# Retention attention and two expert layers on one core: attention's chunk loads held behind the first, decode steps spread later, blend operands in other slots

## The chip, the core and the metric

The kernel runs on one NeuronCore of one Trainium2 chip. The core has a matrix engine (TensorE, "PE" in the profile, with its weight loads as "PEld"), VectorE ("DVE"), ScalarE ("ACT"), GpSimd ("POOL") and SyncE ("SP", which here only issues DMAs). Sixteen DMA engines carry the transfers that the queues of SP, ACT and POOL ask for. Each engine runs its own instruction stream in order; semaphores order the engines among each other. The metric is the device time of one execution in microseconds (us). Three executions of the kernel before took 986.65, 987.84 and 989.09 us.

## The reference, cut to what matters

```python
# attention: 4 batches, 8 heads, 768 tokens, head size 64
for t in range(S):
    state = gamma * state + einsum('bhd,bhe->bhde', k[:, :, t], v[:, :, t])
    y[:, :, t] = scale * einsum('bhd,bhde->bhe', q[:, :, t], state)
x = y.transpose(0, 2, 1, 3).reshape(B * S, H * D)      # 3072 x 512
# first expert layer: w1, w2 are 512 x 1024, w3 1024 x 1024, w_out 1024 x 512
h = (x @ w1) * (x @ w2) @ w3
x = (h @ w_out).astype(float32)
# second: w_in 512 x 2048, w_out 2048 x 512
h = x @ w_in
out = (h * sigmoid(1.702 * h)) @ w_out
```

The weights come as 64-bit floating point numbers.

## The kernel before, in words

**Arithmetic.** Every large product is made of three matmuls in the fast 32-bit format (`mm3`, L245 to L248). Each operand is held as a high part and a low part, the remainder: high x high, high x low, low x high. So each operand needs a cast to its high part on ACT (line L261) and a subtraction for its low part on DVE (L162). The larger products are done in seven block products instead of eight, with sums and differences of blocks as operands.

**Stages, in the order of time.**
- *Attention*: 24 chunks of 128 tokens (four batches of six). A chunk's input is a tile `qkv` with q and k (`qk`) and k and v (`kv`). `scores` makes s (L354), `masked` makes pt on DVE (L366), `updates` and `next_state` hold the running state (the copy on ACT is L392), `outputs` makes y (L404), which DVE turns into xb (L426) and which is split into xh and xl. `load(c)` asks for a chunk: chunk 0's and 1's qk go out on SP's queue (L333), their kv and all later chunks on POOL's (L334, L336). In the preamble the loads of chunks 0 to 5 are asked for one after the other.
- *Gates*: six blocks of 512 tokens (n = 0 to 5), each with eight gates (t = 0 to 7). A gate multiplies a block of x with one tile of w1 and w2 (24 matmuls), and ACT and DVE multiply both results (L284, L285) to a tile of h, which goes to DRAM (`hd`); in n = 3 to 5 with its sums and differences b and g (L1009 to L1015). n = 0 runs among attention's chunks. The x of the next block is reloaded (`reload`) and split in four pieces d = 0 to 3 (`split_x`) during the present one. Among the gates of n = 1 and 2 lie eight "mixes", in which w3 and w_out are multiplied with each other.
- *Blend*: 21 turns, three token blocks times seven products, each 24 matmuls, with h as the operand and the mixed weight; a turn's operand is one megabyte from `hd`, loaded by `load_h` (L790) into a tile l0 to l3, then cast to `h` (ACT) and reduced to its low part (DVE).
- *Expand*: four token blocks by eight tiles of w_in, with the gelu; the left operands (`op`) come from DRAM (`sp`), two tiles each (high and low), in the places that `SLOT` gives them.
- *Contract*: 21 turns that end in the stores to `out`.

**Weights.** A weight tile comes from DRAM as two raw tiles of 64-bit numbers (`fetch`, L118, five buffers). ACT takes its magnitude (L128), DVE rebuilds the 32-bit number in steps (L183 to L205), ACT and DVE split it, or POOL makes sums of it (`seven`, L159). `weight_steps` is a generator with ten such steps a tile; `work(n)` runs the next n. It is called with a number after every gate, every mix and in the first turns of blend, so that the decoding lies between the other instructions of DVE and ACT. An earlier fetch is held by a small memset on DVE (L117) into the raw tile, which the DMA must wait for.

**What sets the order.** Everything is issued in the order of the program text, per engine. Tiles come from pools; a tile that takes another's place waits until that one's last reader is through. The blend's four tiles l0 to l3 lie where the gate stage's last tiles lay: the first on the staging tiles `st`, the second on both `b12`, the third and fourth on the two tiles `g`. The last gates of n = 5 ("opening", L665 on) also load and split what blend's turns 0 and 1 start with.

Of the kernel before, what the change touches and what calls it, by code (L numbers as in the profile page):

```python
# [43 lines left out]
def tile_kernel(  # L44
# [225 lines left out]
    def split_x(key, d):  # L270
        hi, lo = (t[:, d] for t in xhl[key])
        split(hi, lo, lo.bitcast(F32))
# [29 lines left out]
    class Attention:  # L302
# [18 lines left out]
                    t, dyt[0], self.step[:, c].to_broadcast([P, KD, P]), ALU.mult  # L321
                )

        def load(self, c):
            if c in (4, 5):
                qk, kv = (
                    homes["wg"].tile([P, 1024], F32, tag="wg", bufs=16, name=f"c{x}") for x in "qk"
                )
            else:
                t = self.tile("qkv", 2048, 4)  # L330
                qk, kv = t[:, :1024], t[:, 1024:]
            if c in (0, 1, 4, 5):
                (nc.sync if c < 2 else nc.gpsimd).dma_start(qk, qkv[c][:, :1024])  # L333
                nc.gpsimd.dma_start(kv, qkv[c][:, 1024:])  # L334
            else:
                nc.gpsimd.dma_start(t, qkv[c])  # L336
            qkt[c] = qk.rearrange("p (a n t) -> p a n t", a=2, n=NP)
            kvt[c] = kv.rearrange("p (a h d) -> p a h d", a=2, h=H)
# [172 lines left out]
    left = {}  # L511
    PART = dict(P1=0, P2=1, P4=2, P5=3, P6=4, P7=5, P3=6)

    SLOT = "e", 0, 1, 4, 2, 3, 5, 6
    pools = {True: spare}

    def slot(n, shape):
# [207 lines left out]
    def contract(p, ps):  # L725
        def add(out, x, y):
            nc.vector.tensor_tensor(out, x, y, ALU.add)

        def store(x, h, i, q, value):
            t = p.tile([P, TB], F32, tag="o", bufs=4, name="c")  # L730
            add(t, *value)
            at = 0
            while at < TB:
                s, t0 = divmod(i * TB + at, TS)
                m = min(TB - at, TS - t0)
                to = s * 2 * TS + h * TS + t0
                rows = slice((2 * x + q) * P, (2 * x + q + 1) * P)
                nc.sync.dma_start(out[rows, to : to + m], t[:, at : at + m])
                at += m

        u = [p.tile([P, 3, 2, TB], F32, name="ua")]
        for n, (name, i) in enumerate(turns):
            r = n // 3
            load_turn(n + 2, p)
            if i == 0 and r + 1 < 7:
                load_w(turns[n + 3][0], (6, 4)[r % 2], nc.gpsimd if r else nc.sync)
            if name == "P5" and i == 0:
                u += [slot(x, [P, 3, 2, TB]).bitcast(F32) for x in (2, 3)]
            pq = [ps.tile([P, TB], F32, tag="m", bufs=6, name="m") for _ in range(2)]
            for q in range(2):  # L750
                for k in range(NQ):
                    mm3(
                        pq[q],
                        *(t[:, k, q * P : (q + 1) * P] for t in ws[name]),
                        high[n][k // KH][:, k % KH],
                        low_of(n, k),
                        k == 0,
                        k == NQ - 1,
                    )
            split_turn(n + 1, p)  # L760
            if i == 1 and r + 1 < 7:
                split_w(turns[n + 2][0], (7, 5)[r % 2])
            for q, m in enumerate(pq):
                ua, p5, u4 = (t[:, i, q] for t in (u * 3)[:3])
                if name == "P1":
                    nc.scalar.copy(ua, m)
                if name == "P2":
                    store(0, 0, i, q, (m, ua))
                if name == "P6":
                    add(ua, m, ua)  # L770
                if name == "P5":
                    nc.scalar.copy(p5, m)
                    add(u4, ua, p5)
                if name == "P3":
                    store(0, 1, i, q, (m, u4))
                if name == "P7":
                    add(ua, m, ua)
                    store(1, 1, i, q, (ua, p5))
                if name == "P4":
                    store(1, 0, i, q, (m, ua))  # L780
# [6 lines left out]
    def load_h(n, a, b, t):  # L787
        i, name = blends[n]
        lo2.setdefault(n, []).append((a, b, t))
        nc.sync.dma_start(t.bitcast(F32), hd[i][:, a:b, RIGHT[name]])  # L790
# [17 lines left out]
    def opening(t):  # L808
        if t:
            name = blends[t - 1][1]  # L810
            wm[name] = wtile("wg")
            nc.sync.dma_start(
                wm[name][1].bitcast(F32), sm[PART[name]].rearrange("p k c -> p (k c)")
            )
        if t == 1:
            x = spare.tile([P, 7, TB], F32R, tag="ope", name="h0")
            hi2[0] = x[:, NM:]
            load_h(0, 0, NM, x[:, :NM])
        if t == KF - 2:
            for k in (0, 2):  # L820
                load_h(1, k, k + 2, prep.tile([P, 2, TB], F32R, tag="r", bufs=R_BUFS, name="h1"))
        if t in (3, 4, 5):
            split_h(0, t - 3, t - 2, hi2[0][:, t - 3 : t - 2])
        if t == 6:
            hi2["k3"] = prep.tile([P, TB], F32R, tag="x", bufs=6, name="h3")
            split_h(0, 3, 4, hi2["k3"].rearrange("p (a t) -> p a t", a=1))
        if t in (4, 6):
            split_wm(t // 2 - 2)

    def blend(p, ps, todo):  # L830
# [4 lines left out]
        def tile(kind, bufs):  # L835
            return p.tile([P, NM, TB], F32R, tag=kind, bufs=bufs, name=kind)
# [13 lines left out]
        def store(i, e, t):  # L850
            nc.gpsimd.dma_start(yd[i][:, e], t)

        ls = {n: tile(f"l{n % 4}", 1) for n in range(2, 6)}
        for n in (2, 3):
            load_turn(n)
        held = [p.tile([P, TB], F32, tag="o", bufs=2, name="c")]
        hi2[1] = tile("h", 2)
# [48 lines left out]
    with tc.manual_schedule():  # L906
# [4 lines left out]
        with (  # L911
# [8 lines left out]
            nc.sync.dma_start(attention.step[:, :NCK], cstep)  # L920
            attention.factors(0)
            for c in range(2, 6):
                attention.load(c)
            attention.factors(1)
            gates = 0
            late = []
# [7 lines left out]
                gates += 1  # L934

            def fill(c, at):
                for _ in range({(0, 0): 2, (3, 0): 2, (4, 0): 1}.get((c, at), 0)):
                    fetch(held=True)
                if c > 1:
                    work(PACE.get(c, (1, 1, 2, 1))[at])  # L940
                if (c, at) == (CPB + 1, 2):
                    magnitude(1)
                while late:
                    gate_first(*late.pop())
                if c in range(13, 17) and at == 1:
                    reload(ORDER[1], c - 13)
                if c in range(17, 21) and at == 3:
                    split_x(ORDER[1], c - 17)
                if at == 3 and c > CPB + 1 and gates < min(complete, KF):
                    first_gate()  # L950
# [7 lines left out]
        with (  # L958
# [63 lines left out]
            for n, i in list(enumerate(ORDER))[1:]:  # L1022
                nxt = ORDER[n + 1] if n + 1 < NB else None
                for t in range(KF):
# [7 lines left out]
                    if n >= 2 and nxt is not None and t == KF - 2:  # L1032
                        load_b(nxt, 0)
                    ab = gate_mm(t, i, gate_tile)
                    if nxt is not None and t >= KD:
                        split_x(nxt, t - KD)
                    work(((8, 6, 3, 3)[n - 1] + (n < 4) * (t % 2)) if n < 5 else (t < 4) + (t < 5))
                    (gate_second if n > 2 else gate_first)(t, i, ab)
                    while rows < KF and (complete > W3 + rows or (n, t) == (2, KF - 1)):
                        ps = mix_mm(rows)  # L1040
# [149 lines left out]
```

## Time and profile before

| | us |
|---|---|
| three runs, median | 987.84 |
| the profiled execution | 987.63 |
| its span (first to last instruction) | 985.8 |
| PE busy | 965.2 (98%) |
| DVE busy | 716.9 (73%) |
| ACT busy | 444.4 (45%) |
| POOL busy | 200.6 (20%) |

The stages begin at: attention 0, gates of n = 1 138, n = 2 226, n = 3 271, n = 4 316, n = 5 362, blend 405, Expand 521, contract 750. A row of the timeline gives start and duration, the engine, the line, the operation, output <- input, and in brackets how long the engine was idle before, and on whom it waited. PEclk is the TensorE clock granted, as a share of 2.4 GHz; 0.50 is the lower level of 1.2 GHz. The three runs spread over 2.4 us.

### The profile page before, as it was taken

The numbers are of one execution on the slowest core, as the hardware profiler recorded it, in microseconds if no ns is written. First come the engines' busy times: TensorE is split into PE (matmuls) and PEld (weight loads), VectorE is DVE, ScalarE is ACT, GpSimd is POOL, SyncE is SP. The second block draws the span as 40 slices with busy tenths as digits, with TensorE's granted clock in tenths as the row PEclk, the third lists the DMA queues.
The fourth block names the chain that finished last, engine by engine and source line by source line (L and its number), as shares of the span: only waits on it lengthen the run. The fifth ranks groups of instructions, "written<-read, shape, count | busy, mean of one in ns | idle before, by whom it ended". The sixth has DMA issues, their size and how long they took to land.

```text
span 985.8 us, 14859 instructions
## 1 busy us (share of the span) xinstructions
PE 965.2 (98%) x5608; PEld 836.6 (85%) x5608; DVE 716.9 (73%) x966; ACT 444.4 (45%) x786; POOL 200.6 (20%) x243
## 2 busy tenths in 40 slices
PE   5999999999999999999999999999999999999998
PEld 5788878888877888888889999999999888888886
DVE  3878878888898986774886895867777475567662
ACT  4666644442322213445445744545445544354430
POOL 4000000259685875340110000000000000000000
PEclk9999999999999999999999999999999999999999
DMA  8989956669988989998877647455596968767971
GB/s 333 354 321 348 360 195 221 200 218 326 339 302 322 358 311 371 378 315 286 278 238 278 261 168 270 187 223 233 194 358 254 331 230 284 244 197 245 288 232 54
DMA packets 115464, 268.73 MB, mean 273 GB/s; under 512 B 8000, under 2 KB 69568, under 8 KB 106304
## 3 DMA queue, kind: packets, MB, share of 16 engines
q1 hardware_dynamic: 101552, 196.08, 57.7%
q0 software_dynamic: 13840, 71.70, 18.8%
q8 instruction: 44, 0.72, 0.3%
q14 instruction: 28, 0.23, 0.1%
HBM read 165.52 MB, written 102.24 MB: 272 GB/s over the span
## 4 chain that ended last, share of the span: by engine, by line
PE 64%; DVE 2%; issue 0%; ACT 0%; DVEq 0%
PE m L248 12%; PE m L247 12%; PE m L246 12%; PE a L247 4%; PE a L248 4%; PE a L246 4%; PE psm L247 3%; PE psm L248 3%; PE psm L246 3%; PE e L248 2%; PE e L247 2%; PE e L246 2%; PE c L248 1%; PE c L247 1%; PE c L246 1%; DVE g L583 1%
## 5 line engine op out<-in xcount | busy, mean ns | idle before, releaser
L247 PE MATMUL psm<-xl,wh 128*128 128x512 f32 x320 | 125.3, 392 | 2.3 <-DVE xl L162 2.3
L246 PE MATMUL psm<-xh,wh 128*128 128x512 f32 x320 | 125.4, 392 | 0.8 <-ACT xh L261 0.8
L248 PE MATMUL psm<-xh,wl 128*128 128x512 f32 x320 | 125.2, 391 | 0.0
L248 PE MATMUL m<-h,op 128*128 128x512 f32 x320 | 124.5, 389 | 0.0
L246 PE MATMUL m<-h,op 128*128 128x512 f32 x320 | 124.5, 389 | 0.0
L247 PE MATMUL m<-l,op 128*128 128x512 f32 x304 | 118.3, 389 | 0.0
L685 ACT CAST h<-l 128x2048 fp32r<-128x2048 f32 x38 | 72.3, 1915 | 83.3 <-PE m L248 51.3
L686 DVE TENSOR_TENSOR l<-l,h 128x2048 fp32r<-128x2048 f32 x38 | 85.6, 2287 | 21.2 <-ACT h L685 21.2
L247 PE MATMUL a<-yl,op 128*128 128x384 f32 x256 | 85.7, 335 | 0.1
L246 PE MATMUL a<-yh,op 128*128 128x384 f32 x256 | 85.7, 335 | 0.0
L248 PE MATMUL a<-yh,op 128*128 128x384 f32 x256 | 85.6, 334 | 0.0
L691 POOL DMA_DIRECT2D op<-sw x6 | 3.2, 531 | 393.3 <-PE a L248 212.9
L128 ACT ACTIVATE x<-raw 128x512 f32<-128x512 f32 x72 | 46.3, 673 | 74.4 <-DMA raw<-in_wo_dram 40.5
L247 PEld LDWEIGHTS psm<-xl,wh 128*128 128x128 f32 x320 | 60.5, 189 | 15.7 <-DVE xl L162 3.0
L246 PEld LDWEIGHTS psm<-xh,wh 128*128 128x128 f32 x320 | 60.5, 189 | 13.9 <-ACT xh L261 1.2
L248 PEld LDWEIGHTS psm<-xh,wl 128*128 128x128 f32 x320 | 60.4, 189 | 12.5
L246 PEld LDWEIGHTS m<-h,op 128*128 128x128 f32 x320 | 60.1, 188 | 12.4
L248 PEld LDWEIGHTS m<-h,op 128*128 128x128 f32 x320 | 60.1, 188 | 12.4
L247 PEld LDWEIGHTS m<-l,op 128*128 128x128 f32 x304 | 57.1, 188 | 11.9
L246 PE MATMUL m<-h,wh 128*128 128x512 f32 x168 | 65.4, 389 | 0.0
L248 PE MATMUL m<-h,wl 128*128 128x512 f32 x168 | 65.4, 389 | 0.0
L162 DVE TENSOR_TENSOR l<-l,h 128x2048 fp32r<-128x2048 f32 x19 | 43.6, 2293 | 26.2 <-ACT h L261 24.7
(160 smaller groups left out, 2205.2 us busy)
## 6 DMA issues: line engine op xcount, KB each, us to landing
gd<-g SPq DMA_DIRECT2D x32, 1344.0 KB, 4.8
qkv<-in_qkv_dram POOLq DMA_DIRECT2D x20, 1024.0 KB, 8.3
l<-gd SPq DMA_DIRECT2D x26, 768.0 KB, 6.9
l<-hd SPq DMA_DIRECT2D x19, 1024.0 KB, 6.9
raw<-in_w_dram SPq DMA_DIRECT2D x32, 512.0 KB, 5.1
hd<-g POOLq DMA_DIRECT2D x12, 1280.0 KB, 8.8
raw<-in_wo_dram SPq DMA_DIRECT2D x24, 512.0 KB, 6.9
l<-gd SPq DMA_DIRECT2D x24, 512.0 KB, 5.4
```

What stands on the lines that cost most here:

```text
L128: nc.scalar.activation(x, high, AF.Abs, scale=2.0**16)
L162: nc.vector.tensor_tensor(lo, x, hi.bitcast(F32), ALU.subtract)
L246: nc.tensor.matmul(ps, wh, xh, start=start, stop=False, skip_group_check=True)
L247: nc.tensor.matmul(ps, wh, xl, start=False, stop=False, skip_group_check=True)
L248: nc.tensor.matmul(ps, wl, xh, start=False, stop=stop, skip_group_check=True)
L583: nc.vector.tensor_tensor(g[:, x], y, z, ALU.subtract)
L685: nc.scalar.copy(hi, x.bitcast(F32))
L686: nc.vector.tensor_tensor(x, x.bitcast(F32), hi.bitcast(F32), ALU.subtract)
L691: queue.dma_start(t.bitcast(F32), sw[PART[name]])
```

## The change

Seven edits:
1. `load` takes a second argument. For chunk 2 POOL first copies one column of chunk 0's qk into the new tile, so the DMA behind it is asked for when chunk 0's qk has landed.
2. The first two held raw fetches move from the step behind chunk 0's scores to that behind chunk 1's (`fill`).
3. `work` after each gate: in n = 1 to 4 8, 6, 3, 3 steps, without one more at every second gate of n = 1 to 3; in n = 5 3, 3, 3, 2, 2, 0, 0, 0 in place of 2, 2, 2, 2, 1, 0, 0, 0.
4. `split_x` of the next block at t = 3 to 6 in place of 4 to 7.
5. The operand of blend's turn 1 (h1) is no longer loaded into two raw buffers in the opening. The four tiles l are given to turns 1 to 4 in place of 2 to 5, and three turns are loaded at blend's start in place of two.
6. `SLOT`, the places of the left operands in Expand: operand 4 goes to place 5, 5 to 2, 6 to 3.
7. The very last store: the add is made in two parts (128 and 384 columns), each before its DMA, and the second DMA is issued by ACT.

```diff
-        def load(self, c):
+        def load(self, c, behind=None):
...
+                if behind is not None:
+                    nc.gpsimd.tensor_copy(qk[:, :1], behind)
...
-    SLOT = "e", 0, 1, 4, 2, 3, 5, 6
+    SLOT = "e", 0, 1, 4, 5, 2, 3, 6
...
-            add(t, *value)
+            last = (x, h, i, q) == (1, 0, 2, 1)
+            if not last:
+                add(t, *value)
...
-                nc.sync.dma_start(out[rows, to : to + m], t[:, at : at + m])
+                part = slice(at, at + m)
+                if last:
+                    add(t[:, part], *(v[:, part] for v in value))
+                queue = nc.scalar if last and at else nc.sync
+                queue.dma_start(out[rows, to : to + m], t[:, part])
...
-        if t == KF - 2:
-            for k in (0, 2):
-                load_h(1, k, k + 2, prep.tile([P, 2, TB], F32R, tag="r", bufs=R_BUFS, name="h1"))
...
-        ls = {n: tile(f"l{n % 4}", 1) for n in range(2, 6)}
-        for n in (2, 3):
+        ls = {n: tile(f"l{n % 4}", 1) for n in range(1, 5)}
+        for n in (1, 2, 3):
             load_turn(n)
...
-                attention.load(c)
+                attention.load(c, qkt[0][:, 0, 0, :1] if c == 2 else None)
...
-                for _ in range({(0, 0): 2, (3, 0): 2, (4, 0): 1}.get((c, at), 0)):
+                for _ in range({(1, 0): 2, (3, 0): 2, (4, 0): 1}.get((c, at), 0)):
...
-                    if nxt is not None and t >= KD:
-                        split_x(nxt, t - KD)
-                    work(((8, 6, 3, 3)[n - 1] + (n < 4) * (t % 2)) if n < 5 else (t < 4) + (t < 5))
+                    if nxt is not None and t in range(KD - 1, KF - 1):
+                        split_x(nxt, t - KD + 1)
+                    work((8, 6, 3, 3)[n - 1] if n < 5 else (3, 3, 3, 2, 2, 0, 0, 0)[t])
```

The change moves instructions at three places. The first is DVE's queue at the program's start; the memsets on `raw` release the first two fetches of weights. Before:

```order
L366 TENSOR_TENSOR pt<-s,mask 128x512 x2
L117 MEMSET raw 128x2 x2
L366 TENSOR_TENSOR pt<-s,mask 128x512 x2
L426 TENSOR_TENSOR xb<-y,dy 128x512
L162 TENSOR_TENSOR xl<-xb,xh 128x4x128
```

DVE's queue at the same place now:

```order
L368 TENSOR_TENSOR pt<-s,mask 128x512 x4
L428 TENSOR_TENSOR xb<-y,dy 128x512
L162 TENSOR_TENSOR xl<-xb,xh 128x4x128
L117 MEMSET raw 128x2 x2
L368 TENSOR_TENSOR pt<-s,mask 128x512 x2
```

The memsets have moved behind both chunks' masks and the xb and xl of chunk 0.

The second place is DVE's queue in the last two gates of n = 3, where the products that end in L1012 and L1009 belong to gates 5 and 6, and the rows of L162 on xl are the split pieces of the next block. Before:

```order
L1012 TENSOR_TENSOR g<-g,b_3202 128x512
L162 TENSOR_TENSOR xl<-xl,xh 128x512
L191 TENSOR_SCALAR x<-x 128x512
L195 SCALAR_TENSOR_TENSOR x<-raw,x 128x512 x2
L285 TENSOR_TENSOR b_3288<-b_3288,psm 128x512
L1009 TENSOR_TENSOR g<-b_3288,h 128x512
L162 TENSOR_TENSOR xl<-xl,xh 128x512
L205 SCALAR_TENSOR_TENSOR x<-raw,x 128x512 x2
```

DVE's queue now, from gate 4 to the same product of gate 6 (lines are five higher from L1004 on):

```order
L1014 TENSOR_TENSOR g<-b_3173,h 128x512
L162 TENSOR_TENSOR xl<-xl,xh 128x512
L195 SCALAR_TENSOR_TENSOR x<-raw,x 128x512
L205 SCALAR_TENSOR_TENSOR x<-raw,x 128x512 x2
L285 TENSOR_TENSOR g<-g,psm 128x512
L1017 TENSOR_TENSOR g<-g,b_3173 128x512
L162 TENSOR_TENSOR xl<-xl,xh 128x512
L183 TENSOR_SCALAR x<-x 128x512 x2
L191 TENSOR_SCALAR x<-x 128x512
L285 TENSOR_TENSOR b_3264<-b_3264,psm 128x512
L1014 TENSOR_TENSOR g<-b_3264,h 128x512
```

The last xl piece stands behind gate 5's products and no longer behind gate 6's.

The third place is SP's queue at the end of the gates and the start of blend, where the numbers tell apart what has the same name (l1 to l3 are the tiles of blend's operands, wl those of its weights). Before:

```order
L812 DMA wl_3933<-sm0_99 128x1024
L790 DMA h1_3935<-hd0_77 128x2x512
L790 DMA h1_3937<-hd0_77 128x2x512
L812 DMA wl_3976<-sm0_99 128x1024
L790 DMA l2_4022<-hd0_77 128x4x512
L790 DMA l3_4023<-hd0_77 128x4x512
L790 DMA l0_4024<-hd0_77 128x4x512
L790 DMA l1_4025<-hd0_77 128x4x512
L790 DMA l2_4151<-hd0_77 128x4x512
```

SP's queue there now (L798 is the line that was L790, L820 that which was L812):

```order
L820 DMA wl_3914<-sm0_99 128x1024
L820 DMA wl_3953<-sm0_99 128x1024
L798 DMA l1_3999<-hd0_77 128x4x512
L798 DMA l2_4000<-hd0_77 128x4x512
L798 DMA l3_4001<-hd0_77 128x4x512
L798 DMA l0_4002<-hd0_77 128x4x512
L798 DMA l1_4088<-hd0_77 128x4x512
L798 DMA l2_4133<-hd0_77 128x4x512
```

The two halves of h1 are gone, and the four tiles now begin with turn 1's operand.

## Rows read from the trace of the kernel before

**Rows 1.** Windows: length, busy time of each engine, PEclk, DMA share, GB/s

```profile
40.62:981.53 940.91, 936.60 (x5194) 812.54 (x5192) 693.77 (x924) 420.95 (x709) 187.75 (x220) 1.00 0.76 270
318.25:322.00 3.75, 3.75 (x10) 2.93 (x11) 3.71 (x6) 1.16 (x2) 2.46 (x4) 0.54 1.02 425
426.70:443.00 16.30, 16.30 (x73) 13.50 (x72) 12.66 (x11) 7.29 (x5) 7.41 (x11) 1.00 0.95 322
```

**Rows 2.** Waits of PE over the whole span: us in total, times, longest

```profile
PE s L354 <- DMA qkv<-in_qkv_dram: 10.3, 2, 6.0
PE psm L247 <- DVE xl L162: 2.3, 2, 2.0
...
PE psm L246 <- ACT xh L261: 0.8, 1, 0.8
```

**Rows 3.** Timelines of PE, POOL, DVE and ACT, first 25 us

```profile
12.37 2.08 PE L354 MATMUL s<-qkv 64*128 64x128 f32 x16 [6.03 <-DMA qkv<-in_qkv_dram]
...
2.47 1.05 POOL L336 DMA_DIRECT2D qkv<-in_qkv_dram  x2
...
18.63 1.11 DVE L162 TENSOR_TENSOR xl<-xb,xh 128x512 fp32r<-128x512 f32 x1 [0.69 <-ACT xh L261]
...
24.15 1.23 ACT L128 ACTIVATE x<-raw 128x512 f32<-128x512 f32 x2
```

**Rows 4.** DMA from 0 to 7.8: a queue's packets, MB; an issue's landing

```profile
q0 software_dynamic: 267, 1.02, 40.6%
...
ck<-in_qkv_dram POOLq DMA_DIRECT2D x2, 512.0 KB, 17.5
```

**Rows 5.** DMA issues of the page: KB each, us to landing

```profile
raw<-in_w_dram SPq DMA_DIRECT2D x32, 512.0 KB, 5.1
```

**Rows 6.** DMA issues from 27 to 29

```profile
raw<-in_w_dram SPq DMA_DIRECT2D x2, 512.0 KB, 8.9
```

**Rows 7.** Timeline around 318, end of n = 3

```profile
317.48 0.68 DVE L162 TENSOR_TENSOR xl<-xl,xh 128x512 fp32r<-128x512 f32 x1
...
318.22 0.57 PE L247 MATMUL psm<-xl,wh 128*128 128x512 f32 x1 [1.98 <-DVE xl L162]
```

**Rows 8.** Waits of SP's queue, 404 to 423

```profile
SPq L790 <- DVE g L1012: 13.9, 1, 13.9
SPq L790 <- DMA hd<-g: 11.5, 2, 11.2
```

**Rows 9.** Timelines of SP, ACT and DVE, end of the gates and blend

```profile
391.91 0.53 SPq L790 DMA_DIRECT2D l<-hd  x1
...
406.45 1.49 SPq L790 DMA_DIRECT2D l<-hd  x2
...
415.82 0.59 ACT L847 COPY s<-m 128x512 f32<-128x512 f32 x1 [1.56 <-PE m L248]
416.31 1.92 ACT L261 CAST h<-l 128x2048 fp32r<-128x2048 f32 x1
...
418.25 2.29 DVE L162 TENSOR_TENSOR l<-l,h 128x2048 fp32r<-128x2048 f32 x1 [0.75 <-ACT h L261]
...
419.23 0.52 SPq L790 DMA_DIRECT2D l<-hd  x1
...
421.26 0.59 ACT L847 COPY s<-m 128x512 f32<-128x512 f32 x1 [1.62 <-PE m L248]
```

**Rows 10.** DMA issues of 391.5 to 392.5, 404 to 407, 407 to 410, 419 to 419.5

```profile
l<-hd SPq DMA_DIRECT2D x1, 1024.0 KB, 16.0
...
l<-hd SPq DMA_DIRECT2D x1, 1024.0 KB, 6.7
...
l<-hd SPq DMA_DIRECT2D x1, 1024.0 KB, 13.4
...
l<-hd SPq DMA_DIRECT2D x1, 1024.0 KB, 5.5
```

**Rows 11.** Timeline of SP's queue, the end

```profile
982.29 0.81 SPq L738 DMA_DIRECT2D out_dram<-c  x2
```

## Prediction of the time after the change

> **What bounds the kernel now.** I read the page's engine table first, then the waits of PE, the windows, and the timelines around each wait. PE is the engine at its limit. From its first gate at 40.62 us to its last matmul it is busy for 936.60 of 940.91 us [rows 1]. So nothing that makes another engine faster shortens the run, unless PE waits for that engine now, or will. The table of PE's waits [rows 2] says where that can be: 10.3 us for two landings of attention input (4.3 before the first chunk, 6.0 before the second), and 0.8 + 2.3 us in the gates for the two halves of x, xh and xl. A further loss is no wait: behind the longest of these, PE ran at a mean granted clock of 0.54 for 3.75 us [rows 1], which is mostly the lower level of 1.2 GHz, and cost about 3.75 x 0.46 = 1.7 us.
>
> So there are at most some 4.8 us to gain in the gates and the start's landings beside that. Against them stands every place where PE doesn't wait now and the change takes its lead away. The sum goes against the profiled execution, 987.63 us (span 985.8 and 1.8 around it); the median of the runs shown, 987.84, is 0.2 above it.
>
> **x split a gate sooner, with fewer decode steps: -4.8.** The last xl piece of block n = 4 is made by DVE at 317.48, behind two gate products and their decode steps, and PE's first matmul with it starts at 318.22 after 1.98 idle [rows 7]. The change moves that instruction one gate ahead; a gate is 24 matmuls, about 5.4 us (as long as a blend turn, below), more than the 1.98 it was late. It issues no more than before, and the piece that it reads was reloaded two gates or more earlier. The same holds at the start of n = 3, where PE waited 0.77 for xh and 0.31 for xl (0.8 in the table, and 2.3 less 1.98) [rows 2]. The eight decode steps or so that leave the earlier blocks make room on DVE besides. The waits are 3.1, and the slow clock behind the long one is 1.7: 4.8. What is late next at those places is nothing that I find; the next block's edge has no wait today.
>
> Here a rule weighs on the 1.7. The row shows the clock at 0.54 just behind a wait of 1.98, and that is all that this one execution can say. The Trainium skill ("TensorE: Matmul & The Clock Gate", Part 1: The HAM clock gate) holds that the gate watches activity on a free-running beat, so that the same kernel is caught or spared by chance from run to run. By that rule the 1.7 would be missing in some executions of before, and this part would be worth 3.1 there, the whole sum 989.7; I keep the row's value, as the execution that I sum against paid it.
>
> **The first operands of the blend: +4.4.** Before, blend's turn 1 read its operand from two raw buffers loaded during the gates, and the four slots in the new pool served turns 2 to 5. Now those slots serve turns 1 to 4, in the same places, so each operand from turn 2 on gets the slot that the next turn's had. SP's queue shows when these places come free [rows 8, 9]: the first at 391.91; the second and third at 406.45, after SP had stood 13.9 us for the gate stage's last DVE product; the fourth at 419.23, after 11.2 us for the store of g. They landed 16.0, 6.7, 13.4 and 5.5 us later [rows 10]: at 407.9, 413.2, about 420.9 (issued at 407.5) and 424.7.
>
> From landing to use come ACT's cast, 1.92, and DVE's remainder, 2.29 [rows 9]. Turns follow each other at 415.82 and 421.26, 5.44 apart [rows 9].
> - Turn 1: its load no longer has the megabyte of h1 ahead of it, so it lands between 398.6 (7 us, as the faster loads took) and 407.9, DVE can start at 406.4, and it is ready by 408.7 to 412.1, for a turn that begins at 415.82 - 5.44 = 410.4. Cost 0 to 1.7; I take 0, because ahead of it is less than before.
> - Turn 2: lands 413.2, high part 415.1, low part 417.4. Its second matmul needs the low part at 416.0. Wait 1.4.
> - Turn 3: lands 420.9, high 422.8, low 425.1. After turn 2's delay its second matmul would stand at 422.9. Wait 2.2.
> - Turn 4: lands 424.7, low part at 429.0, while it starts at 426.7 + 3.6 = 430.3. No wait.
>
> That is 3.6. The clock may fall behind one of these waits, as it did behind the 1.98, for 1.7 or not at all; I take half, 0.8. Both ends: 0, if the slots come free or the loads land sooner in the new pool; 5.3 with the fall, and with turn 1's 1.7, 7.0. Two more decode steps now lie in each of turns 4 to 7, on tiles as large as an xl piece (0.68 [rows 7]), where DVE is busy for 12.66 of the 16.30 us from 426.7 on [rows 1]; three turns' worth is 4.2 against 3.6 idle. So DVE falls behind there by 0.6 or a little more for a while, but in each turn it makes the next operand ahead of its steps, some 3 us before it is due. No cost.
>
> **The raw fetches at the start: +1.1.** Before, DVE asks for the first two raw weight tiles behind the first masked scores, at 10.1. Now the request stands behind the xl of chunk 0, which ends at 18.63 + 1.11 = 19.7 [rows 3], so the second leaves at about 20.2. ACT reads them in two instructions from 24.15, the second from 24.75, and behind these in its queue stands the copy of the state, for which PE waits. Raw tiles land in 5.1 us in the middle [rows 5], in 8.9 at a crowded place [rows 6], so the second is there at 25.3 to 29.1 and ACT stands 0.5 to 4.3. By then POOL's queue is short: the last half chunk, issued by 5.6, took 17.5 [rows 4] and is in by 23. So I go by the lower row and take 1.1. Less than 0.5 would need a start with nothing else under way.
>
> **Third and later chunks behind the first: 0.** POOL now copies a column of chunk 0 first, so chunk 2's request leaves when that has landed, at about 4.3 (10.3 less 6.0 [rows 2]), and not at 2.47 [rows 3]. But up to 7.8 us POOL's queue had moved 1.02 MB [rows 4], less than the two half-megabytes (1.05 MB) of chunks 0 and 1 that stand before chunk 2 in it. Chunk 2 wasn't under way yet, so it took nothing from chunk 1's landing at 12.37 [rows 3]. Behind the waiting copy stand the later chunk loads alone; the last of them is in by 23 either way, as the queue stays full. Ends: 0.5 lost, if the queue runs dry for a moment, 3.5 gained, if it is really the mere presence of those requests that slows chunk 1.
>
> **The tail: -0.3.** The last add is cut into a quarter and the rest, and the second store goes out on ACT's queue; before, both stores were issued by SP in 0.81 behind the whole add [rows 11]. The second issue, 0.4, now stands beside the first, while a further DVE instruction adds a little. Ends 0 and -0.5. **The other slots** of the left operands cost nothing: the first of them is fetched ahead of Expand and used behind its first products, well after the last blend turn has freed the place.
>
> Sum: 987.63 - 4.8 + 4.4 + 1.1 + 0 - 0.3 = 988.0.
>
> **Rivals.**
> A. The blend isn't late. If the order in which the pools hand out the places lets turns 2 and 3 load 2 us or more sooner, no term of blend is left: 988.0 - 4.4 = 983.6. For it: SP's 13.9 us wait is for a product that moves with the decode load. Against: that product is the last of its stage in either order.
> B. The start gains. Chunk 1 lands up to 3.5 sooner: 984.5. For it: 6.0 us is PE's largest wait, and 1.02 MB by 7.8 is close to the 1.05. The Trainium skill ("DMA: Bandwidth & Descriptors", Queues, rings and completion order) has each DMA engine take packets from its queues in turn, and a queue's in order. By that rule chunk 2 competes only once chunk 1's other half is through, and holding its request back 2 us can't matter while that half is under way: it speaks for 0.
> C. Slower: the raw fetches land late. ACT stands 4.3 at its second raw tile instead of 1.1, the state's copy and PE with it, and the clock falls for 1.7 more: 988.0 + 3.2 + 1.7 = 992.9. It decides from landings over 6 us. For it: that stretch moves chunk inputs at a full share of the engines. Against: the row in the middle.
> D. The split sooner doesn't take the wait away, as ACT's casts are themselves held by raw tiles that come late: 4.8 isn't gained, 992.8.
>
> **How the numbers follow.** Forecast 0.42, A 0.21, B 0.12, C 0.16, D 0.09. What can be told from no change here is about 0.3%, 3 us: 984.9 to 990.8 is the same. The forecast's own range, with blend from 3.6 to 5.3, turn 1 and the tail, is 985 to 991. A is faster nearly whole, B in two thirds, the forecast in a tenth: 0.33. C and D are slower nearly whole, with a tenth of the forecast: 0.27. The same is 0.40. The range goes from 982, past A, to 993, the worse of C and D.
>
> **What would show it.** Right: PE has no wait for xl or xh near 271 and 318 and no half clock there; two waits of 1 to 2.5 us in the blend at its second and third turns, for DVE's l; ACT stands about 1 us at its second raw tile near 25; PE restarts near 12.4 with chunk 1. Wrong: PE restarting before 11.5 (B); blend turns 5.44 apart throughout (A); a PE wait of over 2 us between 25 and 30 (C); psm waits for xl above 0.5 (D).

## The result: 10 us slower, and the profile after

The changed kernel takes 997.45 us in the median of four runs (996.78 to 1000.18), against 987.25 for four of the kernel before (985.85 to 989.09): a ratio of 1.0107, with a 95% interval of 1.0081 to 1.0134. The forecast was 988.0 and its range ended at 993.

The profiled execution took 996.78. From the page of the changed kernel, its span and the row of the engines:

```profile
span 995.0 us, 14853 instructions
...
PE 965.4 (97%) x5608; PEld 835.3 (84%) x5608; DVE 715.6 (72%) x966; ACT 443.9 (45%) x785; POOL 196.9 (20%) x244
```

PE is busy as long as before (965.2) in a span that is 9.2 longer. The waits of PE (us in total, times, longest) say where it stands, and answer to [rows 2]:

```profile
PE s L356 <- DMA qkv<-in_qkv_dram: 8.8, 2, 4.4
PE m L246 <- ACT h L261: 4.5, 1, 4.5
PE y L406 <- DVE xb L428: 3.6, 4, 1.4
PE m L246 <- DVE g L285: 3.1, 1, 3.1
PE m L247 <- DVE l L162: 2.1, 3, 1.5
PE u L382 <- ACT state L394: 1.7, 2, 1.5
```

The rows for xl and xh on psm, the gates' products, are gone, and there are three rows on `m`, the products of blend. Chunk 1's input now costs 4.4 and not 6.0. A table by stages shows it more sharply; its times are those of PE's first matmul of a gate, of blend and of Expand in the timeline, and the span:

| us | to the first gate | gates up to blend | blend | Expand to the end |
|---|---|---|---|---|
| before | 40.6 | 364.1 | 114.2 | 466.8 |
| changed | 41.0 | 358.6 | 128.9 | 466.5 |

Blend without any wait is 21 turns of 5.44, 114.2: before, it had none. So the gates gained 5.5, and blend lost 14.6. The windows of the changed kernel (length, PE busy, then the other engines, PEclk, DMA share, GB/s) show the gain at n = 3 and 4 and the loss at blend's first turns; compare [rows 1]:

```profile
300.00:325.00 25.00, 25.00 (x112) 20.71 (x111) 20.91 (x25) 4.62 (x9) 19.04 (x21) 1.00 0.89 291
402.50:405.60 3.10, 0.00 (x0) 0.00 (x0) 1.29 (x2) 0.59 (x1) 0.00 (x0) 1.00 1.04 436
405.60:410.30 4.70, 4.58 (x12) 3.13 (x12) 0.69 (x1) 0.00 (x0) 3.62 (x3) 0.64 1.00 400
410.30:414.70 4.40, 0.00 (x0) 0.00 (x0) 0.00 (x0) 1.90 (x2) 0.54 (x1) 0.87 1.07 417
414.70:418.00 3.30, 1.72 (x3) 1.11 (x4) 3.27 (x2) 1.92 (x4) 0.00 (x0) 0.50 1.01 420
```

PE stands in the middle of turn 0 and ahead of turn 1, and works at about the lower clock behind both, while the DMA engines are full. Its matmuls' starts give the parts: 3.3 in turn 0 (402.3 to 405.6), 1.7 of slow clock, 4.7 ahead of turn 1 (410.0 to 414.75), 2.1 for its low part, 1.7 of slow clock, 0.9 in two later waits: 14.4 of the 14.6.

The chain that leads there runs over all engines. From the timelines of the changed kernel, 360 to 418 (start, duration, engine, line, output <- input, in brackets the idle time before and its releaser):

```profile
362.53 0.87 SPq L798 DMA_DIRECT2D h<-hd  x1
...
381.93 0.62 ACT L261 CAST h<-h 128x512 fp32r<-128x512 f32 x1 [11.44 <-DMA h<-hd]
...
382.58 0.69 DVE L162 TENSOR_TENSOR h<-h 128x512 fp32r<-128x512 f32 x1 [8.42 <-ACT h L261]
383.19 0.68 DVE L205 SCALAR_TENSOR_TENSOR x<-raw,x 128x512 int32<-128x512 int32 x1
...
383.96 0.85 POOL L159 TENSOR_TENSOR st<-x 128x256 f32<-128x256 f32 x1 [11.59 <-DVE x L205]
...
391.05 1.37 POOL L1018 TENSOR_TENSOR g<-g 128x512 f32<-128x512 f32 x1
...
394.15 0.32 SPq L1004 DMA_DIRECT2D h<-hd  x1
...
394.42 0.56 POOL L1020 DMA_DIRECT2D hd<-g  x1 [0.30 <-POOL g L1019]
...
396.43 0.67 SPq L798 DMA_DIRECT2D l<-hd  x1
...
404.19 0.59 ACT L284 COPY g<-psm 128x512 f32<-128x512 f32 x1 [11.95 <-DMA hd<-g]
404.89 0.68 DVE L285 TENSOR_TENSOR g<-g,psm 128x512 f32<-128x512 f32 x1
405.63 0.50 PE L246 MATMUL m<-h,wh 128*128 128x512 f32 x1 [3.13 <-DVE g L285]
412.80 1.90 ACT L261 CAST h<-l 128x2048 fp32r<-128x2048 f32 x1 [8.02 <-DMA l<-hd]
414.75 0.80 PE L246 MATMUL m<-h,wh 128*128 128x512 f32 x1 [4.54 <-ACT h L261]
```

Read it downwards. The load of h0, turn 0's operand, is asked for at 362.53 and there at 381.9. ACT stands 11.44 us at its first cast, with the gates' products queued behind it. DVE stands for the cast, and the decode step L205 behind it completes a weight tile, so POOL's sums of that tile begin at 383.96, and POOL's g at 391.05 stands behind those. Both go on late: the store of g is issued at 394.42 (387.82 before), so ACT's last gate product waits for that store's tile until 404.19 and PE for the result bank that this frees, 3.1 us. And SP, which waits for POOL's g with the load ahead of l1, issues l1 at 396.43, not at 391.91 [rows 9]; it lands at 412.8, 16.4 us later; its forerunner took 16.0 [rows 10].

These are the rows on SP's side, its waits from 340 to 425 and the landing of h0 among the DMA issues of 361 to 365:

```profile
SPq L1004 <- POOL g L1019: 49.3, 5, 19.4
SPq L798 <- DVE g L1017: 9.2, 1, 9.2
```

```profile
h<-hd SPq DMA_DIRECT2D x1, 1024.0 KB, 19.4
```

The same places in the kernel before: ACT's first cast of h0, h0's landing, and the store of g.

```profile
378.42 0.62 ACT L261 CAST h<-h 128x512 fp32r<-128x512 f32 x1 [2.81 <-DMA h<-hd]
...
h<-hd SPq DMA_DIRECT2D x1, 1024.0 KB, 10.2
...
387.82 0.56 POOL L1015 DMA_DIRECT2D hd<-g  x1 [0.30 <-POOL g L1014]
```

h0's megabyte took 10.2 us before and takes 19.4 now: two raw tiles (1 MB) stand close ahead of it in the queue, and the DMA engines moved 411 GB/s between 370 and 380.

### The profile page after: what moved, and what is told of

Read it like the earlier page. It is cut to its first block, busy times and chain, and to the rows that moved or that the text cites. A ratio compares the mean times of both kernels' runs of the same rounds, so it can differ in the third digit from the quotient of the medians.

```text
span 995.0 us, 14853 instructions
## 1 busy us (share of the span) xinstructions
PE 965.4 (97%) x5608; PEld 835.3 (84%) x5608; DVE 715.6 (72%) x966; ACT 443.9 (45%) x785; POOL 196.9 (20%) x244
## 4 chain that ended last, share of the span: by engine, by line
PE 52%; DVE 3%; issue 1%; ACT 0%; POOL 0%; DVEq 0%
PE m L247 11%; PE m L248 11%; PE m L246 11%; PE a L247 4%; PE a L246 4%; PE a L248 4%; PE e L246 2%; PE e L248 2%; PE e L247 2%; PE c L246 1%; PE c L248 1%; PE c L247 1%; DVE g L585 1%; DVE yl L485 0%; DVE yh L484 0%
## 5 line engine op out<-in xcount | busy, mean ns | idle before, releaser
L688 DVE TENSOR_TENSOR l<-l,h 128x2048 fp32r<-128x2048 f32 x38 | 85.7, 2287 | 20.5 <-ACT h L687 20.5
L162 DVE TENSOR_TENSOR l<-l,h 128x2048 fp32r<-128x2048 f32 x20 | 46.0, 2302 | 34.3 <-ACT h L261 32.8
L246 PEld LDWEIGHTS psm<-xh,wh 128*128 128x128 f32 x320 | 60.1, 188 | 12.6 <-issue 0.2
L246 PEld LDWEIGHTS m<-h,op 128*128 128x128 f32 x320 | 60.1, 188 | 12.6
L248 PEld LDWEIGHTS psm<-xh,wl 128*128 128x128 f32 x320 | 60.0, 188 | 12.6
L248 PEld LDWEIGHTS m<-h,op 128*128 128x128 f32 x320 | 60.1, 188 | 12.3
L247 PE MATMUL m<-l,wh 128*128 128x512 f32 x160 | 63.4, 396 | 2.1 <-DVE l L162 2.1
```

The source lines that it names most:

```text
L162: nc.vector.tensor_tensor(lo, x, hi.bitcast(F32), ALU.subtract)
L246: nc.tensor.matmul(ps, wh, xh, start=start, stop=False, skip_group_check=True)
L247: nc.tensor.matmul(ps, wh, xl, start=False, stop=False, skip_group_check=True)
L248: nc.tensor.matmul(ps, wl, xh, start=False, stop=stop, skip_group_check=True)
L688: nc.vector.tensor_tensor(x, x.bitcast(F32), hi.bitcast(F32), ALU.subtract)
```

## The experiments

Every kernel was timed beside the kernel before on the same chip; a ratio is to that, with its 95% interval. "Blend" is the stage as above, in the profiled execution (114.2 without waits). A chip's kernel before had a median of 987.7 to 989.3.

### Is it h0's landing, or the new tiles by themselves?

`h0_early`: the load of h0 at t = 0, ahead of the two raw tiles.

```diff
-        if t == 1:
+        if t == 0:
             x = spare.tile([P, 7, TB], F32R, tag="ope", name="h0")
```

> The changed kernel with one edit: the load of blend's turn 0 operand (h0) is asked for one gate earlier (t = 0), ahead of the two raw tiles that stand before it in SP's queue in the changed kernel. Theory T (h0's landing after 19.4 us holds ACT 11.4 us at its first cast; by that DVE's decode step, POOL's sums and its g products come 6.6 us late, then the store of g and the load of l1, and PE waits 3.1 + 4.5 + 1.5 us at half clock): h0 is there before ACT comes to it, ACT's wait for h<-hd is under 3 us, the 3.1 us bank wait is gone, turn 1 waits under 2 us; time 986 to 990. Rival R (the tiles l1 to l3 in the new slots are late by themselves, whatever ACT did): ACT's wait goes, but turn 1 still waits 4 us or more for l1 and the time stays at 994 to 997.

Measured 989.75, ratio 1.0018 (1.0004 to 1.0031), blend 120.5. ACT's first cast of h0 in this kernel, from its timeline:

```profile
372.86 0.57 ACT L284 COPY b<-psm 128x512 f32<-128x512 f32 x1
373.32 0.63 ACT L261 CAST h<-h 128x512 fp32r<-128x512 f32 x1
```

It follows the product ahead of it at once: ahead of the raw tiles h0 landed after 9.6 us. The bank wait and the wait of 4.5 are gone.

`h0_split_late`: no transfer moves, ACT's casts of h0 do.

```diff
-        if t in (3, 4, 5):
-            split_h(0, t - 3, t - 2, hi2[0][:, t - 3 : t - 2])
-        if t == 6:
+        if t in (5, 6, 7):
+            split_h(0, t - 5, t - 4, hi2[0][:, t - 5 : t - 4])
+        if t == 7:
```

> The changed kernel with one edit: the four casts of h0 stand two gates later in ACT's queue (t = 5, 6, 7, 7 in place of 3, 4, 5, 6); no transfer is moved. Theory T: ACT reaches the first cast at about 381, when h0 (landing 382) is nearly there, so its wait shrinks from 11.4 to under 2 us and the chain behind it goes: time 986 to 991. If a full DMA queue alone made l1 and the store of g late, and not ACT's standing still, the time stays at 995 to 998.

Measured 988.63, ratio 1.0007 (0.9989 to 1.0025), blend 118.1. From its timelines, ACT's first cast of h0, which no longer waits, and SP's load of l1:

```profile
379.92 0.62 ACT L261 CAST h<-h 128x512 fp32r<-128x512 f32 x1
...
385.78 37.56 SPq L798 DMA_DIRECT2D l<-hd  x7
```

The transfers are the same, in the same order, and h0 lands as slowly (18.9 us), yet l1 is asked for 10.6 us sooner and nearly 9 us come back. So it is ACT's standing still, and not the full DMA queues alone, that made the store of g and l1 late. Blend is still 3.8 us longer than without waits, and 2.7 of that are its PE waits, 380 to 440:

```profile
PE m L247 <- DVE l L162: 2.3, 2, 1.8
PE m L246 <- ACT h L261: 0.4, 1, 0.4
```

`n5_before`: the last block's steps as before, to part ACT's stall from POOL's.

```diff
-                    work((8, 6, 3, 3)[n - 1] if n < 5 else (3, 3, 3, 2, 2, 0, 0, 0)[t])
+                    work((8, 6, 3, 3)[n - 1] if n < 5 else (t < 4) + (t < 5))
```

> The changed kernel with one edit: in the last gate block 2, 2, 2, 2, 1 decode steps, as before, in place of 3, 3, 3, 2, 2 (the earlier blocks keep 8, 6, 3, 3). Theory T in two halves: (1) ACT stands at h0's first cast, (2) DVE's last decode step of a weight tile stands just behind h0's first part, and POOL's sums and stores of that tile (8 us) stand ahead of its g products, so the stall is lengthened on POOL before it reaches the store of g and l1. This kernel has no sums of POOL between the g of gates 1, 3 and 5, so half (2) is gone while h0 can still be late: PE's 3.1 us bank wait is gone, turn 1 waits 0 to 2 us, time 989 to 993. If half (1) does it alone: 996 to 998.

Measured 992.29, ratio 1.0052 (1.0033 to 1.0070), blend 124.1. ACT still stands 10.9 at h0, but POOL has no sums there:

```profile
385.30 1.79 POOL L1018 TENSOR_TENSOR g<-g 128x512 f32<-128x512 f32 x1 [12.53 <-DMA wl<-sm]
```

Its g comes 5.8 us sooner than in the changed kernel, and the wait for the bank is gone. Turn 1 waits 4.8, more than the 0 to 2 that I expected: l1 is late all the same. So about half of the 10 us hangs on POOL's sums behind the stall. The other half is there without them, and `h0_split_late`, which keeps POOL's sums and takes the stall away, has neither half.

### The steps, the tiles and the start, each by itself

`steps_before`: the changed kernel with all decode steps as before (the `work` line restored).

> The changed kernel with the decode steps per gate as before (8, 6, 3, 3 with one more at every second gate of the first three blocks; 2, 2, 2, 2, 1 in the last); x split sooner, the tiles, the start and the tail stay changed. Theory T: the spread of the decode steps put raw fetches and POOL's sums beside h0, so without it h0 lands in about 10 us, ACT doesn't stand, and what is left is 987.3 - 4.8 (split) + 0.4 (start) - 0.3 (tail) + 0 to 4 for turns 2 and 3: 983 to 987. Rival R (tiles alone): turn 1 waits 4 us or more, 991 or more.

Measured 992.4, ratio 1.0047 (1.0027 to 1.0068), blend 118.4. Taking the decode spread out gives back 5 of the 10 us; the rest is there still, more than my theory allowed. In its profile ACT still stands 6.3 at h0, and the first gate comes at 44.1, after 4.3 of waiting for the state. `n5_before`, with the last block's steps alone as before, gave back as much, so what the steps cost lay in that block.

`tiles_only`: the kernel before with the tiles and the left operands' places.

```diff
-    SLOT = "e", 0, 1, 4, 2, 3, 5, 6
+    SLOT = "e", 0, 1, 4, 5, 2, 3, 6
...
-        if t == KF - 2:
-            for k in (0, 2):
-                load_h(1, k, k + 2, prep.tile([P, 2, TB], F32R, tag="r", bufs=R_BUFS, name="h1"))
...
-        ls = {n: tile(f"l{n % 4}", 1) for n in range(2, 6)}
-        for n in (2, 3):
+        ls = {n: tile(f"l{n % 4}", 1) for n in range(1, 5)}
+        for n in (1, 2, 3):
```

> The kernel before with two edits: blend's four tiles serve turns 1 to 4 (no h1 in raw buffers), with the left operands' places that belong to it. Forecast: PE waits 1.4 at turn 2 and 2.2 at turn 3 for l, with 0 to 1.7 of half clock: 991 to 993. Theory now, after the stage from blend's first matmul to Expand's took 118.4 with these tiles against 114.2 before: +4, 991 to 992. If the waits come only when PE is earlier than before, as with the sooner split: 988.

Measured 991.74, ratio 1.0039 (1.0022 to 1.0055). That is +3.9 by the ratio, near the forecast's +4.4. Its make-up differs; the windows of this kernel around turn 2, which starts at 418.1:

```profile
418.00:420.40 2.40, 0.57 (x4) 0.24 (x2) 2.40 (x2) 2.40 (x4) 0.00 (x0) 1.00 0.98 406
420.40:426.00 5.60, 5.60 (x18) 4.43 (x19) 5.60 (x6) 2.81 (x3) 0.00 (x0) 0.70 0.72 246
```

One wait at turn 2, which costs 2.0 by the matmuls' starts, then 5.6 x 0.30 = 1.7 of slow clock, and none at turn 3; together nearly the 3.8 by which blend is longer.

`raws_only` and `chunk_only`: the kernel before with one of the two edits at the start.

```diff
-                for _ in range({(0, 0): 2, (3, 0): 2, (4, 0): 1}.get((c, at), 0)):
+                for _ in range({(1, 0): 2, (3, 0): 2, (4, 0): 1}.get((c, at), 0)):
```

> The kernel before with one edit: the first two raw fetches asked for behind the xl of chunk 0. The forecast said +1.1 (0 to 4.3) for ACT's standing at its second raw tile. Profiles with this edit and the held chunks show PE waiting for the state 0.9, 1.5, 4.0 and 4.3. Theory: the first gate starts 1 to 4 us later than in the kernel before; of that the blend takes some back, as PE comes to it later: 988 to 990. If the two start edits help one another (the raw tiles no longer compete with chunk 1): first gate no later than 40.6, time 987 to 988.

```diff
-                attention.load(c)
+                attention.load(c, qkt[0][:, 0, 0, :1] if c == 2 else None)
```

> The kernel before with one edit: chunk 2's request, and with it those of chunks 3 to 5, waits for chunk 0's qk (POOL's copy). The forecast said 0, between -3.5 and +0.5. The four profiles with this edit and the later raw fetches show chunk 1's scores at 9.9 to 10.9 (before: 12.4 and 12.9) and the first gate between 39.5 and 44.1 (before: 40.6 and 41.6). Theory: chunk 1 lands 2 us sooner, but as the raw fetches keep their place, the first gate starts at 38.5 to 40 and the blend gives part of it back: 986 to 988. By the forecast (chunk 2 isn't under way yet) chunk 1's scores stay at 12.4 or later.

`raws_only` 988.53, ratio 1.0016 (0.9997 to 1.0036); `chunk_only` 988.10, ratio 1.0011 (0.9993 to 1.0029). Neither can be told from nothing. Over all profiles of this study, chunk 1's scores begin at 9.8 to 12.3 in the nine where the later chunks are held (10.9 in the middle), and at 11.4 to 13.2 in the eight where not (12.6), so the edit does bring that landing forward, mostly. But PE then waits for xb, pt and the state: in the changed kernel 1.5 us at 26.5 for the state, behind ACT's late second raw tile, and 1.4 for xb at 40. In the five profiles with both edits that wait for the state was 0.7 to 4.3; in `raws_only`, with chunk 1 at 13.2, there was none at that place. The first gate of the changed kernel is no earlier (41.0, before 40.6); over all profiles it lies between 39.1 and 44.1.

### Where does the gain of the sooner split go?

`split_only`: the kernel before with that edit alone.

```diff
-                    if nxt is not None and t >= KD:
-                        split_x(nxt, t - KD)
+                    if nxt is not None and t in range(KD - 1, KF - 1):
+                        split_x(nxt, t - KD + 1)
```

> The kernel before with one edit: the next block's x split at t = 3 to 6 in place of 4 to 7. PE's waits of 0.8 at n = 3 and 2.0 at n = 4 go, and the half clock behind the second: 987.3 - 4.8 = 982.5; 984.2 if the half clock isn't part of most executions. If the decode steps that stay as they were hold the split as before: 987.

Measured 988.63, ratio 1.0005 (0.9989 to 1.0021): no gain. In its profile the psm waits are gone and the gates take 359.6 and not 364.1, but blend takes 120.5. Its PE waits from 380 to 440, ACT's first cast of h0, and the windows at blend's first turns:

```profile
PE m L247 <- DVE l L162: 3.7, 2, 1.8
```

```profile
382.61 0.62 ACT L261 CAST h<-h 128x512 fp32r<-128x512 f32 x1 [10.58 <-DMA h<-hd]
```

```profile
400.00:410.00 10.00, 10.00 (x46) 8.26 (x44) 6.91 (x7) 4.01 (x5) 5.04 (x4) 1.00 1.04 408
410.00:420.00 10.00, 8.09 (x35) 6.00 (x33) 4.72 (x5) 5.86 (x6) 0.00 (x0) 1.00 1.03 410
```

PE comes 3.6 us sooner to a blend whose loads don't, and ACT stands 10.6 at h0 here too, with the decode steps of before. That is 7.8 longer than before: ACT comes to the cast 3.6 sooner, SP asks for h0 0.4 later (368.63 against 368.18, both behind POOL's g), and its landing takes 14.0 us and not 10.2. Two theories for blend's loads: the loads are paced by the volume of transfers (P), or by the places that come free (Q).

`split_left_later`: `split_only`, with Expand's first left operand (0.92 MB) fetched in turn 8 instead of turn 0.

```diff
-            if n == 0:
+            if n == 8:
                 left_tile(0)
                 fetch_left(0)
```

> split_only (x split a gate sooner; 988.6, with blend 6.3 longer in its profile) with one edit more: the left operand of Expand (0.92 MB, op<-sp, needed at the end of blend) is fetched by POOL in turn 8 and not in turn 0. Theory P (the start of blend is paced by transfers: the DMA engines are full from 390 to 420 in split_only, so what PE gains before is given back in waits for l): turn 3's operand lands about 2.3 us sooner (0.92 MB at 400 GB/s), the wait at turn 3 goes, time 985.5 to 987.5. Rival Q (the waits come from the places of l3 and l0 coming free late): no change, 988 to 989.

Measured 986.5, ratio 0.9972 (0.9959 to 0.9986), blend 118.7, with the wait of turn 3 gone. That is what P expected and Q did not.

`extra_megabyte`: the kernel before with two loads of 512 KB that nothing reads.

```diff
+            if t > 5:
+                nc.sync.dma_start(
+                    wm[name][0].bitcast(F32), sm[PART[name]].rearrange("p k c -> p (k c)")
+                )
```

> The kernel before with one edit: two loads of 512 KB that nothing reads (the high halves of blend's last two mixed weights, overwritten by their casts later) stand ahead of h1's second use, in gates 6 and 7 of the last block. Theory P (the start of blend is paced by transfers, and the kernel before stands just at that limit): 1 MB at 400 GB/s is 2.6 us, the kernel before has 1.6 to 2.3 us between landing and use at turns 2 to 4, so PE waits 0.5 to 2.6 and the time is 988.8 to 991 (with half clock behind a wait). Rival Q (only the places of l3, l0 and l1 set the pace): no change, 988.3.

Measured 990.12, ratio 1.0008 (0.9996 to 1.0020), blend 114.5: no wait of blend that could be told. It is inconclusive, as PE came to blend 3 us later in this profile than in that of the kernel before (gates 367.1, with 4.4 of psm waits and their slow clock), which gave the loads more time.

`split_left_casts`: `split_left_later` with the casts of h0 two gates later, as in `h0_split_late`.

> split_left_later (986.5) with one edit more: the four casts of h0 two gates later (t = 5, 6, 7, 7). There ACT still stood 11.2 us at h0's first cast, and the store of g and the loads behind it came late. If that stall costs blend the 2 to 4 us that are left (its stage took 118.7 against 114.2 without waits): 983 to 985. If what is left is the volume of the transfers alone: 986 to 987.

Measured 983.21, ratio 0.9934 (0.9919 to 0.9949), 6 us under the kernel before on its chip. All PE waits of this kernel behind 42 us:

```profile
PE y L404 <- DVE xb L426: 0.9, 1, 0.9
PE a L246 <- ACT u L551: 0.3, 1, 0.3
PE psw L248 <- DVE wl L137: 0.2, 1, 0.2
PE u L380 <- ACT state L392: 0.2, 1, 0.2
```

Gates 359.2, blend 114.2: the split's gain is whole at the end, once ACT doesn't stand at h0 and the left operand is out of the way. What the split alone lost was therefore ACT's stall and the volume, about half each: by the ratios the later left operand gave 3.3 us and the later casts 3.8 more. The casts alone were not tried on `split_only`, so this division holds in this order only.

`split_all_later`: with the last two mixed weights' loads behind l2's, and the last store in two parts.

> split_left_casts with two edits more: the last two mixed weights' loads behind l2's and the last store in two parts with ACT's queue (tail, -0.26 in the changed kernel's profile). Theory P: h1 and l2 land up to 1.3 us sooner each: 982 to 984.5. If not: 0.3 under split_left_casts, for the tail.

Measured 983.32, ratio 0.9934 (0.9917 to 0.9950): the same as without. The order of the weights' loads is worth nothing there; the tail's 0.3 is below what can be told.

Three kernels built on the changed one went the same way, with less gain. They keep its tiles, which is the likely reason, though no run parts these from the decode steps that they keep as well. `late_casts_early_raws` (late casts of h0; raw fetches as before) was expected as follows:

> The changed kernel with two edits: h0's casts two gates later (which brought it from 997.5 to 988.6), and the first two raw fetches back behind the first scores. In the profiles with the later raw fetches PE waited 0.9 to 4.3 for the state, behind ACT's reads of the raw tiles, and the first gate came at 39.5 to 44.1. Theory: without that wait the first gate comes at 38.5 to 40, and the time is 986 to 987.5, as the blend (paced by its loads) gives part back. Rival: the earlier raw tiles hold chunk 1 up again; no gain, 988.6.

It took 987.12, ratio 0.9994 (0.9985 to 1.0004). With the last two mixed weights behind l1, `weights_behind_l1`:

> late_casts_early_raws with one edit more: the loads of blend's last two mixed weights (wl, 512 KB each, needed from turn 5 on) stand behind the load of l1 in SP's queue and not ahead of it. Theory P (the blend's start is paced by transfers: the DMA engines are full from 370 to 400, and what PE gains before is given back there): l1 lands about 2.5 us sooner (1 MB at 400 GB/s), l2 and l3 as before, and the time falls by 1 to 2.5 us against late_casts_early_raws. Rival Q (the blend waits for the places of l2 and l3 to come free, that is for the gates' last products and the store of g, and not for bandwidth): l1 lands sooner, turns 2 and 3 wait as before, no change within 0.5 us.

986.55, ratio 0.9986 (0.9970 to 1.0002), not to be told from the one before. With the left operand in turn 8 besides, `all_moves`:

> weights_behind_l1 (986.6) with one edit more: Expand's left operand fetched in turn 8 and not in turn 0. Theory P: turn 2's and 3's operands land up to 2.3 us sooner, blend's stage falls from 120.6 towards 118, time 984 to 985.5. Rival Q: 986 to 987.

985.78, ratio 0.9972 (0.9959 to 0.9985); blend 119.3, not the 118 that P would have, so in these kernels P is not borne out to its size.

## Why the prediction was wrong, by its own steps

Two steps failed: turn 1's operand, priced at 0 to 1.7, and the decode steps of the last gate block, which had no price. In their place the runs show one chain: ACT's wait of 11.4 us at h0, lengthened on POOL, made the store of g and the load of l1 late, and blend lost 14.6.

- **x split: -4.8.** Right at its place: the waits and the half clock are gone, and the gates take 5.5 less. Wrong was the sentence "What is late next at those places is nothing that I find; the next block's edge has no wait today". I asked it of the next gate block and not of blend's start, where turn 4's operand could be there by 425.1 (landing, cast, remainder) for a use at 426.7, and where ACT already stood 2.8 us at h0. `split_only` gives it all back there, and `split_left_casts` keeps it.
- **Turn 1: 0.** This step failed. I bounded it at 0 to 1.7 with l1 issued at 391.91 as its forerunner was, "because ahead of it is less than before". What stood ahead of it was SP's wait for POOL's g, and that came 6.6 us later, so that l1 was asked for 4.5 later. Nor did it land faster for having less ahead of it: 16.4 us against 16.0. It cost 6.8 (4.7 + 2.1) and slow clock, with 3.3 more in turn 0 by the same g.
- **The decode steps** had a price in blend, "No cost", and none in the last gate block, where three a gate replace two. There they put the step that releases POOL's sums behind h0's first part. (The two raw tiles ahead of h0 come from the thinner steps of the blocks before: `n5_before` has them too, and h0 took 18.8 there.) The order shows this without a run; DVE, before and then changed:

```
L205 SCALAR_TENSOR_TENSOR x<-raw,x 128x512 x2
L285 TENSOR_TENSOR b_3810<-b_3810,psm 128x512
L1009 TENSOR_TENSOR g<-b_3810,h 128x512
L162 TENSOR_TENSOR h_3729<-h_3729 128x512
```

```
L162 TENSOR_TENSOR h_3705<-h_3705 128x512
L205 SCALAR_TENSOR_TENSOR x<-raw,x 128x512
```

  `steps_before` puts all of it at 5 us, and `n5_before` the last block's alone at as much.
- **Turns 2 and 3: +4.4.** Right in size by itself (+3.9 us by the ratio of `tiles_only`), with one wait and its slow clock in place of two waits.
- **Raw fetches: +1.1, chunks: 0.** The first is about right in the changed kernel (PE waited 1.5 for the state; up to 4.3 in other profiles with both edits, as rival C feared), but `raws_only` didn't have that wait, so the term isn't shown for that edit alone. The second was too firm: chunk 1 came 1.5 sooner in the changed kernel. "Chunk 2 wasn't under way yet" was read from the time up to 7.8, and chunk 1's scores began at 12.37; POOL's queue in the kernel before, from 7.8 to 12.3:

```profile
q0 software_dynamic: 217, 1.50, 79.2%
```

  With the 1.02 MB up to there that is well past the two half-megabytes, so chunk 2 was under way in those last 4 us. The Trainium skill ("DMA: Bandwidth & Descriptors", Queues, rings and completion order), by whose turn-taking between queues I held the landing to be the same, doesn't settle it; the starts of 10.9 against 12.6 in the middle of nine and eight profiles do. What in the held requests brings them forward stays open. Both together made the first gate 0.4 later.
- **Tail: -0.3.** From the last matmul's start to the end 4.66 before, 4.40 now: -0.26.
- Of the rivals none had the mechanism. D came nearest, in that ACT's casts were held by a load, but at h0 and not at xl. B's sign came true (PE restarts before 11.5: at 10.86), but not its gain, as PE then waited elsewhere before the first gate.
- **The clock.** I had weighed the Trainium skill's rule ("TensorE: Matmul & The Clock Gate", Part 1: The HAM clock gate) that the gate's watch is free-running, so that the slow stretch of one kernel varies from run to run. In the profiles of `raws_only`, `tiles_only` and `extra_megabyte`, where PE again waited 2.1 to 2.9 for that xl, PEclk in the 3 us behind was 0.50 to 0.52, as before (0.55): there the fall came with the wait. What did vary by execution was the wait, which `chunk_only` didn't have at that place. But in blend, of ten waits of 1.8 to 1.9 for l over all profiles, eight were followed by the lower clock and two were not. These two, the 3 us behind the wait in `split_only` (turn 2) and in `h0_split_late`:

```profile
414.30:417.30 3.00, 3.00 (x13) 2.46 (x14) 2.28 (x3) 0.00 (x0) 0.00 (x0) 1.00 1.02 414
406.40:409.40 3.00, 2.98 (x13) 2.49 (x14) 3.00 (x4) 3.00 (x4) 0.00 (x0) 1.00 1.06 394
```

  So the length of a wait doesn't decide the fall by itself; that fits the Trainium skill's rule and doesn't prove it.

What stays open: why h0 takes 14.0 us to land in `split_only`, where no raw tiles stand just ahead of it, beyond that the engines are full (405 GB/s from 370 to 380, before 404); and the single executions of one kernel spread over up to 10 us, so terms of 1 us at the start stay unproven.

## What to carry to other kernels

When a change makes the bounding engine earlier at one place, look at the next place where it meets a transfer, and compare its lead there with the gain: a lead of 2 us can pass on 2 us at most, and in `split_only` a gain of 4.5 us in the gates left nothing at the end. An in-order engine that waits for one load holds everything queued behind it; before a step is moved, see on each engine which wait it now stands behind, and which other engine's queue it releases. Put a cast of an early-loaded operand as late in its engine's queue as its use allows: here two gates of delay were worth nearly 9 us in one kernel and nearly 4 in another.

## What was not expected of the hardware

One megabyte of the same form (h0) took 10.2 us in one kernel and 19.4 in the other, both at about 400 GB/s in all: here its landing was set by what else was under way far more than by its size. Nor that PE's clock, behind a wait of 1.8 us in mid-stream (`tiles_only`), would cost nearly as much again, 1.7, and behind a wait as long in `h0_split_late` nothing.
